# Sliding-window attention beside a squared-ReLU MLP: second products placed between first products, and attention values written to consecutive rows

## The chip, the cores and the metric

The kernel runs on one core of one Trainium2 chip, in float32 throughout; matrix products take their operands as pairs of a rounded high part and a low part. The metric is device time in microseconds. A core has five engines with instruction queues of their own: TensorE (PE in the profile; its weight loads are PEld), VectorE (DVE), ScalarE (ACT), GpSimd (POOL) and SyncE (SP). All transfers of this kernel are issued by SP, in program order.

## The reference

For 2048 tokens of 640 features, with 32 heads of 20 features and a window of 256 keys:

```python
xn = layernorm(x)
q, k, v = split(xn @ wqkv)                     # 32 heads, Dh = 20
scores = (q @ k.T) * 20 ** -0.5                # kept where 0 <= i - j < 256
s = (softmax(scores) @ v) @ wo
r = relu(xn @ w1 + b1)                         # F = 1536
g = silu((r * r) @ w2 + b2)
out = x + s * g
```

## The kernel before, in words

**Phase one** (to about 116 us of the profile) normalizes x, transposes it, spills it in halves (`xs`), forms all values V and the first group of queries and keys.

**The main loop** (L1133, to about 784 us) has 267 steps: 16 pairs of heads times 16 tiles of 128 queries, and 11 steps of lag. A step holds scores of one pair and tile (`sps`, L478), their row maxima on VectorE (L486), the transposed scores of nine steps earlier (`stps`, L518), their exponentials on ScalarE (`p`, L524) and the masks of these on GpSimd (L525, L527). Every fourth step also turns four tiles of row maxima (L493) on TensorE, rounds them on ScalarE (`row` L499, `mrow` L500), forms the low part on GpSimd (L501), and two DMAs write them into two rows of the queries (`qs<-mrow`, L503), so that the transposed scores come with the maximum already subtracted. Every fourth step also multiplies exponentials by V (`ops`, L546); the result goes through ScalarE (`osb`, L551) to DRAM (`o`, L552, issued at L564). The rest of TensorE's time is filled, from a generator, with other products: at first queries and keys (`qkps`), then the MLP.

**The MLP** runs in eight blocks: two halves of F times four groups of 512 tokens. A block has six first products (`hps`: `th` 0 and 1, two halves of the block's tokens, times `fp` 0 to 2) of 30 matmuls each, 256 columns wide, and eight second products (`yps`: tile `tt` 0 to 3 times half `nh` of the output features) of 18 matmuls each, 320 wide. A first product is evacuated by two relu (L930) and two squares (`hh`, L932) on ScalarE, two squares on VectorE that read the bank again (`sq`, L936), and two subtractions on GpSimd (`hl`, L937). A second product with `tt` 0 or 1 reads the three pairs (`hh`, `hl`) of `th` 0, for each half of F's chunks in the order `hh`, `hh`, `hl`. It leaves its bank by one addition on VectorE (L968); the tile goes to DRAM.

**Lanes and banks.** Every product is done in two halves of 64 rows of the array, which run beside each other: a front half of one product with a back half of the product before it. A half without a partner takes a slot alone. All products share three banks of PSUM. The back lane is a product behind the front lane, so a product's bank becomes free only when its back halves and its evacuation are done.

**What sets the order.** All engines' orders are as written by the program. A planner's clock adds up assumed costs of matmuls; `later(wait, f)` writes `f`'s instructions when that clock has advanced by `wait`; `ps.free(after)` says when a bank counts as free again; `room()` makes the filler wait for that. A second product is written once the piece it reads is in `made`, that is, once the instructions that make it have been written. Weight pieces (`wraw`) are loaded a few steps ahead and split on ScalarE (L767) and VectorE (L770); `ensure` (L738) forces what is not yet split. Bulk transfers (weights, `xb`, the next pair's queries and keys) go out at two places of a step, by `issue` (L671).

**The tail** (from 794 us) is the output projection (`wops`, L599): eight units of two tiles. For each unit, sums and unnormalized values come back from `o` (L1026, L1027) and `y` (L1029), VectorE divides (L1040, L1044), and the product is multiplied by the gate (`res`, L1098), added to x on GpSimd (L1103) and written out (`out_dram`).

## Time and profile before

| | |
|---|---|
| median of 3 runs | 875.52 us (875.32 to 877.31) |
| profiled execution | 873.83 us |
| its span | 872.1 us |
| granted TensorE clock, mean | 0.996 |
| TensorE busy | 853.6 us (98%), 10640 matmuls |
| VectorE, ScalarE, GpSimd busy | 497.1, 401.0, 332.0 us |
| DMA | 168.60 MB, mean 193 GB/s |

Times of single instructions come from one profiled execution. Matmuls overlap in TensorE's pipeline: the time from one start to the next counts, not the length of one. A row of the timeline gives start, length, engine, line, operation, output and inputs, and in brackets how long the engine was idle before it and what released it.

### The profile page before, as it was taken

How to read it: one execution, taken by the hardware profiler on the slowest of the kernel's cores; microseconds unless marked ns; L12 is line 12 of the kernel's file. 1: busy time of each engine (PE TensorE's matmuls, PEld its weight loads, DVE VectorE, ACT ScalarE, POOL GpSimd, SP SyncE). 2: the span in 40 equal slices, each digit the busy share in tenths (PEclk: the TensorE clock that was granted, in tenths of full speed). 3: DMA queues.
4: the chain of work that ended last, by engine and by line, in shares of the span. 5: the costliest groups of instructions: out<-in, count | busy, mean ns of one | idle time of the engine just before them, and what ended most of it. 6: DMA issues, size and time to landing. Idle time of an engine off the chain costs nothing.

```text
span 872.1 us, 26728 instructions
## 1 busy us (share of the span) xinstructions
PE 853.6 (98%) x10640; PEld 796.5 (91%) x10640; DVE 497.1 (57%) x1448; ACT 401.0 (46%) x800; POOL 332.0 (38%) x700
## 2 busy tenths in 40 slices
PE   9999999999999999999999999999999999999998
PEld 8999999888888999989989989998989999999998
DVE  7652146656567755555655566764655555536764
ACT  5222114545556744644644654743643644653231
POOL 6010002333333643643543543642543543541343
PEclk9999999999999999999999999999999999999999
DMA  7997578787788546245348346367348256157995
GB/s 268 310 399 276 173 205 264 252 256 232 256 275 287 128 144 177 70 138 187 78 129 249 85 114 182 98 196 214 85 129 244 81 148 200 50 163 236 288 296 172
DMA packets 92901, 168.60 MB, mean 193 GB/s; under 512 B 9448, under 2 KB 41320, under 8 KB 91752
## 3 DMA queue, kind: packets, MB, share of 16 engines
q1 hardware_dynamic: 92776, 166.89, 62.1%
q8 instruction: 84, 1.38, 0.7%
q14 instruction: 41, 0.34, 0.1%
HBM read 94.71 MB, written 71.57 MB: 191 GB/s over the span
## 4 chain that ended last, share of the span: by engine, by line
PE 86%; DMA 7%; DVE 2%; issue 2%; ACT 1%; POOL 1%; SPq 0%; DVEq 0%; POOLq 0%; ACTq 0%
PE yps L468 19%; PE hps L468 18%; PE qkps L468 13%; PE ops L546 9%; PE vps L228 8%; PE stps L518 5%; PE wops L599 4%; PE sps L478 4%; DMA qs<-mrow 4%; PE qkps L205 3%; DMA out_dram<-res 2%; DMA vp<-v_d 1%; POOL res L1103 1%; PE tps L172 1%; DVE junk L486 0%
## 5 line engine op out<-in xcount | busy, mean ns | idle before, releaser
L486 DVE CUSTOM_DVE_ANT_0 junk<-sps,mask 128x384 bf16<-128x384 f32 (+2 forms) x512 | 272.3, 532 | 211.4 <-PE sps L478 57.6
L524 ACT ACTIVATE p<-stps 128x768 f32<-128x768 f32 (+2 forms) x256 | 197.8, 773 | 291.8 <-PE stps L518 240.9
L468 PE MATMUL yps<-w,hh 64*128 64x320 f32 x1536 | 229.3, 310 | 5.1 <-DVE sq L936 4.7
L525 POOL TENSOR_SCALAR_AFFINE_SELECT p<-p 128x256 f32<-128x256 f32 x256 | 105.9, 414 | 333.0 <-ACT p L524 329.8
L468 PE MATMUL hps<-xb,w 64*128 64x256 f32 x2520 | 218.5, 284 | 0.0
L468 PEld LDWEIGHTS hps<-xb,w 64*128 64x128 f32 x2520 | 207.0, 188 | 5.5 <-issue 5.4
L468 PEld LDWEIGHTS yps<-w,hh 64*128 64x128 f32 x1536 | 181.5, 185 | 11.3 <-DVE sq L936 6.2
L468 PE MATMUL yps<-w,hl 64*128 64x320 f32 x768 | 172.4, 309 | 0.0
L478 PE MATMUL sps<-ks,qs 60*128 60x384 f32 (+2 forms) x512 | 140.9, 342 | 0.8 <-DVE mt L486 0.5
L518 PE MATMUL stps<-qs,ks 62*128 62x384 f32 (+2 forms) x512 | 132.8, 334 | 4.9 <-DMA qs<-mrow 4.8
L468 PEld LDWEIGHTS yps<-w,hl 64*128 64x128 f32 x768 | 112.3, 185 | 1.8 <-issue 1.7
L468 PE MATMUL qkps<-xT,wgkh 64*128 64x512 f32 x320 | 100.9, 395 | 0.0
L468 PE MATMUL qkps<-xT,wgqh 64*128 64x512 f32 x320 | 99.2, 393 | 0.0
L546 PE MATMUL ops<-p,vp 128*21 128x128 f32 (+1 forms) x2112 | 92.8, 313 | 0.0
L527 POOL TENSOR_SCALAR_AFFINE_SELECT p<-p 128x256 f32<-128x256 f32 x224 | 92.7, 414 | 0.0
L518 PEld LDWEIGHTS stps<-qs,ks 62*128 62x128 f32 x512 | 85.8, 188 | 7.4 <-issue 7.0
L478 PEld LDWEIGHTS sps<-ks,qs 60*128 60x128 f32 x512 | 86.0, 186 | 2.9 <-DVE mt L486 1.7
L546 PEld LDWEIGHTS ops<-p,vp 128*21 128x21 f32 x2112 | 65.2, 100 | 22.0 <-issue 8.8
L937 POOL TENSOR_TENSOR hl<-sq,hh 128x256 fp32r<-128x256 f32 x96 | 71.0, 756 | 24.5 <-ACT hh L932 21.9
L228 PE MATMUL vps<-wv,xT 128*128 128x320 f32 x480 | 71.5, 308 | 0.0
L228 PEld LDWEIGHTS vps<-wv,xT 128*128 128x128 f32 x480 | 70.5, 188 | 0.1
L599 PE MATMUL wops<-wo,oT 128*128 128x320 f32 x384 | 63.2, 314 | 2.1 <-DVE res L1098 1.4
(100 smaller groups left out, 1188.0 us busy)
## 6 DMA issues: line engine op xcount, KB each, us to landing
ks<-k_d SPq DMA_DIRECT2D x64, 240.0 KB
qs<-q_d SPq DMA_DIRECT2D x64, 240.0 KB
xb<-xs SPq DMA_DIRECT2D x60, 256.0 KB
xs<-xT SPq DMA_DIRECT2D x8, 1280.0 KB
y<-ysb SPq DMA_DIRECT2D x32, 320.0 KB
k_d<-shm SPq DMA_DIRECT2D x19, 512.0 KB
q_d<-shm SPq DMA_DIRECT2D x19, 512.0 KB
o<-osb SPq DMA_DIRECT2D x64, 128.0 KB
```

Source lines behind the costliest of these rows:

```text
L205: nc.tensor.matmul(ps, wt[:, c, :], xT[part][b][:, c * BT + t0:c * BT + t0 + n], start=m == 1, stop=m == 3 * KC)
L228: nc.tensor.matmul(ps, xT[xp][b][:, c * BT + t * P: c * BT + (t + 1) * P], wv[wp][:, c, nh * HALF:(nh + 1) * HALF], start=first and m == 0 ...
L468: return nc.tensor.matmul(out, a[r], b_[r], skip_group_check=True, **kw)
L478: nc.tensor.matmul(ss[hh][:, :nk], qs[i][o, q * P:(q + 1) * P], ks[i][o, k0 * P:k0 * P + nk], start=True, stop=True)
L486: nc.vector.tensor_tensor_reduce(out=junk[:, :nk], in0=ss[hh][:, :nk], in1=mask[:, 3 * P - nk:], scale=1.0, scalar=-3.0e38, op0=ALU.add, o ...
L518: nc.tensor.matmul(tps[:, hh, :n], ks[i][o, kb * P:(kb + 1) * P], qs[i][o, kb * P:kb * P + n], start=True, stop=True)
L524: nc.scalar.activation(p32[:, :, :n], tps[:, :, :n], AF.Exp, scale=SCALE)
L525: nc.gpsimd.affine_select(p32[:, :, 0:P], p32[:, :, 0:P], pattern=[[0, 2], [1, P]], compare_op=ALU.is_ge, fill=0.0, base=0, channel_multip ...
L527: nc.gpsimd.affine_select(p32[:, :, 2 * P:], p32[:, :, 2 * P:], pattern=[[0, 2], [-1, P]], compare_op=ALU.is_gt, fill=0.0, base=0, channel ...
L546: nc.tensor.matmul(ot[r0:r0 + VW, c0:c0 + len(part), :], vps[p][:, kb // 4, kb % 4, hh, :], pt[:, hh, :].rearrange("p (t n) -> p t n", n=P ...
L599: nc.tensor.matmul(ps, a, b_, start=j == 0, stop=j == n - 1)
L937: nc.gpsimd.tensor_sub(hh[1][:, sls[i]], sq, f32(hh[0][:, sls[i]]))
```

## The change

- **Order of products.** Before, a block had its six first products, then its eight second products. Now the second products of its first tile lie between the first products of its second pass: h(0,0), h(0,1), h(0,2), h(1,0), y(0,0), h(1,1), y(0,1), h(1,2), then y(1,0) to y(3,1). The forced splitting of w2 and the first loads of `yin` move with y(0,0), to a place two products earlier; `late` is called only from `tt` 1 on.
- **Both squares together.** The two `sq` and `hl` of a first product are written at one time, 0.8 after relu, in place of 0.6 and 1.0; the bank counts as free 1.0 later, in place of 0.7.
- **Rows of the output write.** `o` has the layout [16 pairs, 128 rows, 256], so that a write goes to 128 consecutive rows. In the tail, each unit's sums and values come by eight loads of 32 partitions in place of two of 128.
- **Bulk transfers.** The rule that held them back in every fourth step (up to the row-maximum DMAs) and in the step before it is gone; a piece of `xb` costs 0.4 of the rate, in place of 0.8.

```diff
-    o_d = [dram.tile([2 * 32, H, MT], F32, name=f"o_{g}") for g in range(NB)]
+    o_d = [dram.tile([NP, P, MT], F32, name=f"o_{g}") for g in range(NB)]
...
-            post(o_d[g][:, 2 * p:2 * p + 2, :].rearrange("r h n -> h r n"), osb.rearrange("p e n -> p (e n)"))
+            post(o_d[g][p], osb.rearrange("p e n -> p (e n)"))
...
     def issue(amount):
-        if state[2] % 4 == 3 or state[2] % 4 == 0 and not rowed[0]:
-            return
         credit[0] = min(credit[0] + amount, amount)
...
-        its = [bulk_dma(0.8, f32(xb[p])[:, c], xs_d[p][b][:, c]) for p in range(2) for c in cs]
+        its = [bulk_dma(0.4, f32(xb[p])[:, c], xs_d[p][b][:, c]) for p in range(2) for c in cs]
...
+            def first(th, fp):
...
                         def rest(i):
                             sq = at2.tile([P, MT], F32, tag="sq", name="sq")
                             nc.vector.scalar_tensor_tensor(sq, ps.tile[:, sls[i]], b1t[:, fi + i:fi + i + 1], rs[i], ALU.add, ALU.mult)
                             nc.gpsimd.tensor_sub(hh[1][:, sls[i]], sq, f32(hh[0][:, sls[i]]))
                             if i:
                                 made.add((th, fp))
-                                ps.free(0.7)
-                        later(0.6, lambda: rest(0))
-                        later(1.0, lambda: rest(1))
+                                ps.free(1.0)
+                        later(0.8, lambda: (rest(0), rest(1)))
...
-            if n % NB == 0:
-                ensure(f"2{hf}")
-            if n == NB:
-                load_yin(0)
-                load_yin(1)
-            wt2 = w2t[hf]()
-            for tt in range(4):
...
+            def second(tt, nh):
+                if (tt, nh) == (0, 0):
+                    if n % NB == 0:
+                        ensure(f"2{hf}")
+                    if n == NB:
+                        load_yin(0)
+                        load_yin(1)
+                    wt2[0] = w2t[hf]()
                 t = b * 4 + tt
+                yield from room()
+                if n == last and tt:
+                    late(2 * tt + nh)
...
+            for fp in range(NFH // 2):
+                yield from first(0, fp)
+            for fp in range(NFH // 2):
+                yield from first(1, fp)
+                if fp < 2:
+                    yield from second(0, fp)
+            for tt in range(1, 4):
                 for nh in range(2):
-                    yield from room()
-                    if n == last:
-                        late(2 * tt + nh)
-                    job = start(nh)
-                    for fc in range(NFH):
-                        yield from product(job, nh, fc)
+                    yield from second(tt, nh)
...
-        rows = o_d[u // 2][32 * (u % 2):32 * (u % 2 + 1)]
-        nc.sync.dma_start(sums, rows[DH].unsqueeze(0).to_broadcast([4, H, MT]))
-        nc.sync.dma_start(ob, rows[:DH].rearrange("(c k) h n -> (k h) c n", k=4))
+        rows = o_d[u // 2].rearrange("p (h r) n -> (p h) r n", h=2)[:, 32 * (u % 2):32 * (u % 2) + VW]
+        for k in range(4):
+            nc.sync.dma_start(sums[32 * k:32 * k + H], rows[:, DH])
+            nc.sync.dma_start(ob[32 * k:32 * k + H], rows[:, k:DH:4])
```

**TensorE at the end of a block's third first product.** Before, in the third block: `hps_6894` is that product, the two others are the next two. Its `hl` is `hl_7177`, read for the first time 173 rows further on.

```order
L468 MATMUL hps_6894<-xb0_1_6157,w1_0_1_3364 128x256
L468 MATMUL hps_7027<-xb0_1_6157,w1_0_2_3540 128x256
L468 MATMUL hps_6894<-xb1_1_6158,w1_0_1_3364 128x256
L468 MATMUL hps_7169<-xb0_1_6157,w1_0_0_3362 128x256
L468 MATMUL hps_6894<-xb0_1_6157,w1_0_2_3540 128x256
L468 MATMUL hps_7169<-xb1_1_6158,w1_0_0_3362 128x256
```

Now, in the same block, `hps_6928` is the third first product, `yps_7193` the first second product, and `hh_6955` and `hl_6956` belong to the block's first first product:

```order
L468 MATMUL hps_6928<-xb1_1_6328,w1_0_1_3364 128x256
L468 MATMUL yps_7193<-w2_0_0_3931,hh_6955 128x320
L468 MATMUL hps_6928<-xb0_1_6327,w1_0_2_3540 128x256
L468 MATMUL yps_7193<-w2_0_1_3933,hh_6955 128x320
L468 MATMUL yps_7193<-w2_0_0_3931,hl_6956 128x320
L468 MATMUL yps_7193<-w2_0_0_3931,hh_6955 128x320
```

The third row is the last half of `hps_6928`. Thirty-one rows further on, the same product reads what `hps_6928` leaves, `hh_7199` and `hl_7200`:

```order
L468 MATMUL yps_7193<-w2_0_1_3933,hh_7199 128x320
L468 MATMUL hps_7044<-xb0_1_6327,w1_0_1_3364 128x256
L468 MATMUL yps_7193<-w2_0_2_4087,hh_7199 128x320
L468 MATMUL hps_7044<-xb1_1_6328,w1_0_1_3364 128x256
L468 MATMUL yps_7193<-w2_0_1_3933,hl_7200 128x320
```

The distance from a third product's last half to the first use of its `hl` goes from 173 rows to 31, of which 14 are of `yps_7193`, the others back halves of `hps_7044` and one step's scores.

**ScalarE in the fifth block, where w2 of the second half of F is forced.** Before, the forced pieces (`w2_1_1`, L767) stand ahead of the sixth first product's relu:

```order
L524 ACTIVATE p32_9997<-stps_9988 128x768
L499 ACTIVATE row_10001<-stps_9988 8x128
L500 ACTIVATE mrow_10002<-row_10001 8x128
L767 ACTIVATE w2_1_1_9615<-raw_9783 128x640
L524 ACTIVATE p32_10063<-stps_10056 128x768
L767 ACTIVATE w2_1_1_9615<-raw_9813 128x640
L930 ACTIVATE relu_10090<-hps_9810,b1t_108 128x256
L930 ACTIVATE relu_10092<-hps_9810,b1t_108 128x256
```

Now three of them stand, with a row-maximum step, ahead of the third first product's relu (`hps_9730`), whose results y(0,0) reads next:

```order
L524 ACTIVATE p32_9960<-stps_9951 128x768
L499 ACTIVATE row_9964<-stps_9951 8x128
L500 ACTIVATE mrow_9965<-row_9964 8x128
L765 ACTIVATE w2_1_0_9636<-raw_9654 128x640
L765 ACTIVATE w2_1_1_9638<-raw_9839 128x640
L765 ACTIVATE w2_1_1_9638<-raw_9895 128x640
L927 ACTIVATE relu_9998<-hps_9730,b1t_108 128x256
L927 ACTIVATE relu_10000<-hps_9730,b1t_108 128x256
L929 ACTIVATE hh_9996<-relu_9998 128x256
L929 ACTIVATE hh_9996<-relu_10000 128x256
```

**SP at the start of the tail.** The last write of `o` and the first unit's loads, before:

```order
L1026 DMA sums<-o_85 128x1x256
L1027 DMA ob_14435<-o_85 128x5x256
L1029 DMA yb_14436<-y_84 128x2x640
L564 DMA o_86<-osb 2x64x256
L751 DMA raw<-in_A_wo_dram 32x640 x8
L877 DMA yin<-y_83 128x640
```

and now:

```order
L564 DMA o_86<-osb 128x256
L1027 DMA sums<-o_85 32x256
L1028 DMA ob_14486<-o_85 32x5x256
L1027 DMA sums<-o_85 32x256
L1028 DMA ob_14486<-o_85 32x5x256
L1027 DMA sums<-o_85 32x256
L1028 DMA ob_14486<-o_85 32x5x256
L1027 DMA sums<-o_85 32x256
L1028 DMA ob_14486<-o_85 32x5x256
L1030 DMA yb_14487<-y_84 128x2x640
```

The write's shape is 128x256 in place of 2x64x256, and a unit has nine loads in place of three.

More of the change, by code (lines that the diff above doesn't have):

```diff
@@ L665, in lin1 @@
         return tiles[t][:, o:o + n]
-    bulk, rowed = [], [False]
+    bulk = []
     credit = [0.0]
     def issue(amount):
-        if state[2] % 4 == 3 or state[2] % 4 == 0 and not rowed[0]:
-            return
         credit[0] = min(credit[0] + amount, amount)
@@ L988, in product @@
                     for hp, wp in ((0, 0), (0, 1), (1, 0)):
[L989 to L990 removed]
+                        m += 1
+                        halves(job, ps, hs[tt // 2, fc // 2][hp][:, fc % 2 * MT + tt % 2 * P:fc % 2 * MT + (tt % 2 + 1) * P], lin1(wt2[0], (wp * NFH + fc) * D + nh * HALF, HALF), m == 1, m == 3 * NFH)
                         yield 0.133
[L992 to L998 removed]
+            for fp in range(NFH // 2):
[5 more added lines that the diff above has]
+            for tt in range(1, 4):
+                for nh in range(2):
+                    yield from second(tt, nh)
             if n < last and nxt:
@@ L1133, in attn_mlp_kernel @@
         for s in range(steps):
-            state[2], rowed[0] = s, False
+            state[2] = s
             vload[0] = 0.2 * (s % 4 == 0) + 0.5 * (s % 4 == 3)
```

97 lines of the change are left out of this document (45 added, 52 removed).

## The prediction

> **What bounds the kernel now.** I read the page first, then the waits, then stretches of the timeline. The page (busy time per engine, then the granted clock and DMA share in 40 slices):
>
> ```profile
> PE 853.6 (98%) x10640; PEld 796.5 (91%) x10640; DVE 497.1 (57%) x1448; ACT 401.0 (46%) x800; POOL 332.0 (38%) x700
> PEclk9999999999999999999999999999999999999999
> DMA  7997578787788546245348346367348256157995
> ```
>
> TensorE is busy 98% of 872.1 us at nearly full clock. Nothing else is near a bound on average; DMA reaches it only in the last slices. So an edit can pay only by removing TensorE gaps, half-filled slots or a slow clock, and costs by adding them. The waits (engine, line waited for: us in total, times, longest) say which gaps there are:
>
> ```profile
> PEld yps L468 <- DVE sq L936: 6.2, 6, 1.5
> PE yps L468 <- DVE sq L936: 4.7, 5, 1.3
> PEld yps L468 <- DVE ysb L968: 1.7, 5, 0.6
> PE yps L468 <- DVE ysb L968: 0.3, 1, 0.3
> PEld stps L518 <- issue: 7.0, 8, 1.8
> PE stps L518 <- DMA qs<-mrow: 4.8, 6, 1.6
> DVE res L1098 <- DMA out_dram<-res: 9.6, 6, 4.2
> PE wops L599 <- DVE res L1098: 1.4, 3, 0.8
> ```
>
> Gap A is a second product (yps) waiting for a bank that first products (hps) leave: between 5.0 (matmul rows) and 7.9 us (weight-load rows); I take 7. Gap B is the transposed scores (stps) waiting for the row maxima that come back by DMA: between 4.8 and 7.0; I take 6. Gap C is in the output projection, 1.4 us or somewhat more; I take 1.5.
>
> One A in full, on ScalarE, VectorE and TensorE (start, us, engine, what; in brackets the idle time before it):
>
> ```profile
> 503.93 0.28 PE L468 MATMUL hps<-xb,w 64*128 64x256 f32 x1
> 504.66 0.81 ACT L524 ACTIVATE p<-stps 128x768 f32<-128x768 f32 x1 [1.01 <-PE stps L493]
> 505.37 0.25 ACT L499 ACTIVATE row<-stps 8x128 f32<-8x128 f32 x1
> 505.65 0.31 ACT L500 ACTIVATE mrow<-row 8x128 fp32r<-8x128 f32 x1
> 505.87 0.81 ACT L930 ACTIVATE relu<-hps,b1t 128x256 f32<-128x256 f32 x2
> 507.40 1.42 POOL L937 TENSOR_TENSOR hl<-sq,hh 128x256 fp32r<-128x256 f32 x2 [0.68 <-ACT hh L932]
> 507.71 0.56 PE L468 MATMUL yps<-w,hh 64*128 64x320 f32 x4 [1.27 <-DVE sq L936]
> ```
>
> The last hps half starts at 503.93, but its relu starts 1.94 us later, behind the exponentials and the two row-maximum pieces of that step.
>
> One B, and what stands ahead of it in the DMA queue (SP rows; windows with PE, PEld, DVE, ACT, POOL busy, granted clock, DMA share, GB/s):
>
> ```profile
> 314.75 0.54 SPq L564 DMA_DIRECT2D o<-osb  x1
> 317.22 1.43 SPq L503 DMA_DIRECT2D qs<-mrow  x2
> 315.90:319.30 3.40, 3.40 (x51) 3.40 (x50) 1.66 (x7) 2.08 (x4) 1.30 (x4) 1.00 0.14 41
> 605.42 0.44 PE L518 MATMUL stps<-qs,ks 62*128 62x384 f32 x2 [1.60 <-DMA qs<-mrow]
> 606.50:610.00 3.50, 3.50 (x36) 3.41 (x34) 0.94 (x3) 1.09 (x3) 0.77 (x2) 0.51 0.46 109
> ```
>
> The output write of the attention values, 128 KB, is alone in flight in the first window: 0.14 of 16 engines is 2.2 engines, 41 GB/s, so 128 KB needs about 3.2 us. The small row-maximum DMA is queued behind it. The worst B (1.6 us before 605.42) is followed by 3.5 us at half clock (0.51): 1.7 us more lost.
>
> **The change, part by part.** The sum is made against the profiled execution, 873.8 us (span 872.1 and 1.7 outside it); the median of the runs is 875.5, 1.7 above it, and I add that at the end.
>
> *Rows of the output write.* From 2x64x256 to 128x256: with more engines it no longer blocks the row maxima. B goes from 6 to 0.3 (what is left where transfers of xb now precede it): **-5.7**. If the write stays as it is, 0; if all goes, -7.0. The stretch at half clock behind the worst B goes with it: -1.7.
>
> The Trainium skill, DMA: Bandwidth & Descriptors, section "Why a DMA increments its semaphore by 16 and not by 1", says that a DMA runs on the largest k up to 16 that divides the slowest dimension of both sides: 2 before and 16 now. The 2.2 engines above agree. By that rule 128 KB would take an eighth of its 3.2 us, and B goes wholly; by the row alone I could not tell how many engines the new shape gets.
>
> *Order of products: bank waits.* Alternating kinds removes most hand-overs from hps to yps with a long evacuation. In the new order two stay right behind a row-maximum step, at about 1.4 each (as the 1.27 above), four smaller ones at about 0.35, and the yps-to-yps ones stay at 1.0: 5 in place of 7, **-2** (-4 if the small ones vanish, 0 if none shrinks).
>
> *Order of products: the new wait.* The first second product of a block now starts when the third first product has only just ended. Its 15th front half reads hl of that product, 14 halves after that product's last half on TensorE. What a second-product half costs in a slot of its own (chain of waits, then two timeline pieces with their successors):
>
> ```profile
> 785.87 7.54 PE yps L468 x76
> 788.28 0.56 PE L468 MATMUL yps<-w,hh 64*128 64x320 f32 x4
> 788.57 0.42 PE L468 MATMUL yps<-w,hl 64*128 64x320 f32 x2
> 788.72 0.56 PE L468 MATMUL yps<-w,hh 64*128 64x320 f32 x4
> 790.15 0.45 PE L468 MATMUL yps<-w,hh 64*128 64x320 f32 x2
> 790.44 0.31 PE L468 MATMUL yps<-w,hl 64*128 64x320 f32 x1
> 790.59 0.45 PE L468 MATMUL yps<-w,hh 64*128 64x320 f32 x2
> ```
>
> Six halves in 0.44 us when paired (788.28 to 788.72), three when alone (790.15 to 790.59): 0.147 a slot either way. So 14 slots are 2.06 us, with one pair of scores 2.2. How long hl takes, at its quickest, and what a forced weight piece takes:
>
> ```profile
> 437.76 0.28 PE L468 MATMUL hps<-xb,w 64*128 64x256 f32 x1
> 438.07 0.84 ACT L930 ACTIVATE relu<-hps,b1t 128x256 f32<-128x256 f32 x2 [0.25 <-PE hps L468]
> 439.65 0.74 POOL L937 TENSOR_TENSOR hl<-sq,hh 128x256 fp32r<-128x256 f32 x1 [0.36 <-ACT hh L932]
> L767 ACT ACTIVATE w<-raw 128x640 fp32r<-128x640 f32 x12 | 8.7, 726 | 0.0
> ```
>
> From the last half's start (437.76) to the end of the first hl (440.39) is 2.63 us: 0.4 more than the 2.2 there are. The second hl half takes another 0.74, and is read only 0.44 later: 0.7 in all at the quickest. In blocks 3, 5 and 7 a whole row of attention work lies between (some 4 us), and nothing waits. The five others, by what stands ahead of relu on ScalarE: block 1 nothing, 0.7; block 0 the exponentials (0.7) and the values' copy (0.3), 1.5; blocks 2 and 6 a row-maximum step as at 504.66, where hl came 4.18 after the last half (503.93 to 508.11), of which the new place is 0.7 later in the step, 1.2 each; block 4 the same and three forced pieces of w2 (3 x 0.73), 3.4. Together **+8.0**. From below: only the 0.4 five times, +2; from above: eight blocks at the 504.66 case without its 0.7 (4.2 - 2.2 = 2.0), +16. I take 8, since the order gives each block's queue. Behind the waiting half are queued all of TensorE's work, its back lane too: scores, row maxima and exponentials of the next step are late by the same, so it's paid in full. The 3.4 in block 4 is more than the stall that went before 606.5, so I expect a stretch at half clock behind it: +1.7, which cancels the one removed.
>
> Page TensorE: Matmul & The Clock Gate of the Trainium skill, Part 1 on the HAM clock gate, asks for an idle window of about 3.4 us before the clock halves. The trace differs: 1.6 us idle came before the 0.51 at 606.5. By the rule the stall in block 4 is just long enough for one such stretch, and the sum would be the same.
>
> *Order of products: lanes.* A half without a partner takes the slot of two. After the last values there were 77 halves in 50 slots (7.54 us); by the new order 100 halves in 68: 18 x 0.147 = +2.6. In the loop 35 more halves are alone (+2.3), and 20 of yps move out to the end (-1.5): +0.8. **+3.4**; if partners turn up, 0.
>
> *Both squares together, bank said free later; gate on bulk transfers gone.* One VectorE piece earlier, one bank promise 0.3 later: no term but those above. Transfers of xb now precede the row-maximum DMAs in four steps; that's in the 0.3.
>
> *Tail loads.* A unit's two loads become eight. SP rows of unit three, and C's place:
>
> ```profile
> 816.13 0.54 SPq L1026 DMA_DIRECT2D sums<-o  x1
> 816.77 0.51 SPq L1027 DMA_DIRECT2D ob<-o  x1
> 827.63 0.49 DVE L1098 TENSOR_TENSOR res<-wops,yb 128x320 f32<-128x320 f32 x1 [1.04 <-DMA out_dram<-res]
> SPq L1063 <- POOL res L1103: 33.2, 7, 5.5
> 820.00:850.00 30.00, 29.16 (x196) 28.37 (x194) 20.76 (x29) 8.83 (x10) 12.25 (x12) 1.00 0.98 302
> ```
>
> Eight issues for two are at most 6 x 0.54 = 3.2 us more on SP, which sits idle there 33.2 us in seven waits for GpSimd, 4.7 each: hidden; without that cover 3.2 a unit would delay the output writes. DMA is full (0.98), and the output writes land late for VectorE (1.04 before 827.63). The sums are read to four copies; if they spread like the other loads the queue is shorter and C goes: **-1.5** (0 to -2).
>
> Sum: -5.7 -1.7 -2 +8.0 +1.7 +3.4 -1.5 = +2.2: 876.0 in a profiled execution, **877.7 as the median**.
>
> **The rivals.** *Slower, by the wait for hl.* If hl is late in all eight blocks by an average of 1.6 (between 0.7 and 2.0), that's 12.8, 4.8 more than my term: 882.5. For it: VectorE holds the row maxima ahead of sq. Against it: the 4 us in three blocks. It decides from 0.4 us beyond my 8.0, since 878.1 is 0.3% over 875.5.
>
> *Faster: hl is hardly waited for.* If what stands ahead of relu is done by then, because earlier stalls let ScalarE catch up, 2.5 remains of 8.0, and no slow clock follows: 877.7 - 5.5 - 1.7 = 870.5. For it: ScalarE is 46% busy. Against it: relu was late by 1.94 at 505.87.
>
> *The tail loads are slower.* The new loads read 1 KB pieces at a distance of 64 KB. If they take twice as long, the full DMA queue gives back what the sums save; C stays: 879.2.
>
> The Trainium skill's DMA page, section "Latency and other measured facts", reports copies slowed at row pitches of 512 KiB and above that are powers of two. The pitch here is smaller; no run shows it yet.
>
> *The row maxima stay late.* With the gate gone, xb transfers go out right ahead of them: at four steps 1 us each, 4: 881.7.
>
> **How the numbers follow.** Forecast 0.42, slower by hl 0.22, faster 0.19, tail loads 0.09, maxima late 0.08. About 0.3% (2.6 us) is what a measurement can tell from no change: 872.9 to 878.1. Faster: 0.18 of the faster case and 0.03 of the forecast, **0.21**. Same: 0.28 of the forecast, 0.01, 0.02, 0.04 and 0.02 of the others, **0.37**. Slower: 0.11, 0.20, 0.05 and 0.06, **0.42**. The forecast's own range is 874 to 881; with the other cases' centres and a little beyond, **870 to 884**.
>
> **What would show it.** In the changed profile: no wait of stps for qs<-mrow above 0.5 us, and the lone write's window at a DMA share far above 0.14; waits of yps for POOL's hl (or ScalarE's hh) of about 8 us in five places, the longest in block 4 with a clock near 0.5 behind it; waits of yps for sq of about 4; about 10 us of yps after the last values; DVE's wait for out_dram under 3 us. It is wrong if the hl waits are under 4 or over 11, or if stps still waits 4 us.

## The result

The changed kernel is slower: median 897.1 us of 4 runs (893.7 to 901.9) against 875.4 (874.3 to 877.3) for the kernel before, a ratio of 1.0261 (95% interval 1.0233 to 1.0289). The forecast was 877.7, the range 870 to 884. The profiled execution took 893.7, its span is 892.0; it was 872.1.

The page of the changed kernel (busy time, granted clock and DMA share in 40 slices):

```profile
PE 863.2 (97%) x10640; PEld 801.1 (90%) x10640; DVE 495.7 (56%) x1448; ACT 399.9 (45%) x800; POOL 329.8 (37%) x700
PEclk9999999999999999999999999999999999998999
DMA  7996678779788263174265345274275263066995
```

The same matmuls, and a place near the end where the clock dips and TensorE is less than full. The waits on the way, as they were shown for the kernel before:

```profile
PEld yps L468 <- DVE sq L933: 7.2, 12, 1.4
PE yps L468 <- DVE sq L933: 3.7, 7, 1.1
PEld yps L468 <- DVE ysb L967: 8.5, 4, 7.6
PE yps L468 <- DVE ysb L967: 7.6, 2, 7.4
PEld yps L468 <- POOL hl L934: 8.3, 12, 1.8
PE yps L468 <- POOL hl L934: 5.9, 7, 1.6
DVE res L1099 <- DMA out_dram<-res: 9.3, 6, 4.4
PE wops L599 <- DVE res L1099: 3.5, 5, 0.8
```

Transposed scores no longer wait for the row maxima (no such line is left). The waits for hl are there, 5.9 us by TensorE's matmul rows and 8.3 by its weight-load rows. New and not forecast is one wait of 7.4 us for `ysb`, the addition that empties a second product's bank. On VectorE and TensorE (in brackets the idle time before):

```profile
789.94 0.81 DVE L774 TENSOR_TENSOR wo<-raw,wo 128x640 fp32r<-128x640 f32 x1
796.00 0.83 DVE L774 TENSOR_TENSOR wo<-raw,wo 128x640 fp32r<-128x640 f32 x1 [5.24 <-ACT wo L773]
796.74 1.75 DVE L1041 RECIPROCAL sums<-sums 128x256 f32<-128x256 f32 x1
802.38 0.96 DVE L109 TENSOR_TENSOR oT<-ob,oT 128x768 fp32r<-128x768 f32 x1 [0.91 <-ACT oT L108]
803.25 0.82 DVE L774 TENSOR_TENSOR wo4l<-raw,wo4h 128x640 fp32r<-128x640 f32 x1
803.99 0.88 DVE L967 TENSOR_TENSOR ysb<-yps,yin 128x320 f32<-128x320 f32 x2
804.53 0.90 PE L468 MATMUL yps<-w,hh 64*128 64x320 f32 x4 [7.38 <-DVE ysb L967]
```

VectorE is idle for 5.24 us, waiting for a piece of wo; then it divides the tail's first unit (796.74 to 803.3) and splits the last piece of wo; only then does the addition run, and TensorE goes on. In the kernel before, the addition that mattered stood ahead of the division:

```profile
784.10 0.49 DVE L968 TENSOR_TENSOR ysb<-yps,yin 128x320 f32<-128x320 f32 x1 [2.15 <-PE yps L468]
785.24 1.75 DVE L1040 RECIPROCAL sums<-sums 128x256 f32<-128x256 f32 x1
791.76 0.88 DVE L968 TENSOR_TENSOR ysb<-yps,yin 128x320 f32<-128x320 f32 x2
```

The windows of the changed kernel (stretch, length, then PE, PEld, DVE, ACT, POOL busy, granted clock, DMA share, GB/s) show the stall, a slow clock behind it, and the tail:

```profile
793.50:804.60 11.10, 3.72 (x42) 3.45 (x39) 6.96 (x9) 4.44 (x6) 0.00 (x0) 0.86 0.76 232
804.60:812.76 8.16, 7.43 (x48) 6.93 (x49) 1.40 (x4) 0.95 (x1) 0.00 (x0) 0.77 0.26 83
812.76:890.00 77.24, 72.06 (x480) 70.37 (x480) 49.06 (x69) 18.48 (x21) 30.25 (x30) 1.00 0.86 247
```

By stage, from the profiled executions (start of the span to the last matmul of the values, from there to the first `wops`, the tail to the span's end):

| | before | changed | difference | forecast |
|---|---|---|---|---|
| to the last values | 785.6 | 792.1 | +6.5 | +1.1 |
| last values to the tail | 8.5 | 20.7 | +12.2 | +2.6 |
| tail | 78.0 | 79.2 | +1.2 | -1.5 |

So three fifths of the loss lie in the few microseconds ahead of the tail.

### The profile page after: what moved, and what is told of

It reads as the page before. It is cut to its first block, busy times and chain, and to the rows that moved or that the text cites. A ratio compares the mean times of both kernels' runs of the same rounds, so it can differ in the third digit from the quotient of the medians.

```text
span 892.0 us, 26811 instructions
## 1 busy us (share of the span) xinstructions
PE 863.2 (97%) x10640; PEld 801.1 (90%) x10640; DVE 495.7 (56%) x1448; ACT 399.9 (45%) x800; POOL 329.8 (37%) x700
## 4 chain that ended last, share of the span: by engine, by line
PE 85%; DMA 4%; issue 3%; POOL 2%; DVE 2%; ACT 2%; SPq 2%; POOLq 0%; DVEq 0%; ACTq 0%
PE yps L468 19%; PE hps L468 18%; PE qkps L468 13%; PE ops L546 10%; PE vps L228 8%; PE stps L518 5%; PE sps L478 4%; PE qkps L205 3%; PE wops L599 3%; DMA out_dram<-res 2%; DMA sums<-o 1%; DVE sq L933 1%; ACT p L524 1%; POOL res L1104 1%; PE tps L172 1%
## 5 line engine op out<-in xcount | busy, mean ns | idle before, releaser
L468 PE MATMUL yps<-w,hh 64*128 64x320 f32 x1536 | 272.7, 314 | 12.8 <-DVE ysb L967 7.6
L468 PE MATMUL hps<-xb,w 64*128 64x256 f32 x2520 | 255.0, 284 | 0.0
L468 PEld LDWEIGHTS hps<-xb,w 64*128 64x128 f32 x2520 | 238.5, 188 | 4.9 <-issue 4.7
L525 POOL TENSOR_SCALAR_AFFINE_SELECT p<-p 128x256 f32<-128x256 f32 x256 | 105.3, 411 | 345.3 <-ACT p L524 334.0
L468 PEld LDWEIGHTS yps<-w,hh 64*128 64x128 f32 x1536 | 206.1, 187 | 21.8 <-DVE ysb L967 8.5
L468 PE MATMUL yps<-w,hl 64*128 64x320 f32 x768 | 193.5, 314 | 5.9 <-POOL hl L934 5.9
L478 PE MATMUL sps<-ks,qs 60*128 60x384 f32 (+2 forms) x512 | 138.3, 342 | 0.4 <-DVE mt L486 0.4
L468 PEld LDWEIGHTS yps<-w,hl 64*128 64x128 f32 x768 | 121.3, 187 | 10.7 <-POOL hl L934 8.3
L527 POOL TENSOR_SCALAR_AFFINE_SELECT p<-p 128x256 f32<-128x256 f32 x224 | 91.0, 406 | 0.0
L478 PEld LDWEIGHTS sps<-ks,qs 60*128 60x128 f32 x512 | 83.9, 186 | 3.1 <-DVE mt L486 1.6
```

Source lines behind the costliest of these rows:

```text
L468: return nc.tensor.matmul(out, a[r], b_[r], skip_group_check=True, **kw)
L478: nc.tensor.matmul(ss[hh][:, :nk], qs[i][o, q * P:(q + 1) * P], ks[i][o, k0 * P:k0 * P + nk], start=True, stop=True)
L525: nc.gpsimd.affine_select(p32[:, :, 0:P], p32[:, :, 0:P], pattern=[[0, 2], [1, P]], compare_op=ALU.is_ge, fill=0.0, base=0, channel_multip ...
L527: nc.gpsimd.affine_select(p32[:, :, 2 * P:], p32[:, :, 2 * P:], pattern=[[0, 2], [-1, P]], compare_op=ALU.is_gt, fill=0.0, base=0, channel ...
```

## The experiments

Each was timed beside the kernel before on its chip. Stages as above; "halves" are the second-product halves that TensorE still had to do after the last values.

| | median | ratio (95%) | to last values | to the tail | halves | tail |
|---|---|---|---|---|---|---|
| before | 874 to 875 | | 785.6 | 8.5 | 77 | 78.0 |
| changed | 897.1 | 1.0261 (1.0233 to 1.0289) | 792.1 | 20.7 | 100 | 79.2 |
| e1_late_load | 897.5 | 1.0246 (1.0204 to 1.0288) | 795.0 | 20.1 | 100 | 80.9 |
| e2_last_block_old | 886.2 | 1.0122 (1.0078 to 1.0167) | 790.0 | 12.2 | 100 | 81.3 |
| e3_old_order | 877.4 | 1.0027 (1.0007 to 1.0047) | 778.8 | 17.9 | 89 | 79.6 |
| e4_rows_only | 868.5 | 0.9939 (0.9915 to 0.9964) | 776.1 | 8.5 | 77 | 82.0 |
| f1_division_behind | 894.6 | 1.0218 (1.0186 to 1.0250) | 790.9 | 17.3 | 100 | 82.9 |
| f2_two_writes | 864.2 | 0.9870 (0.9840 to 0.9899) | 776.2 | 8.5 | 77 | 78.1 |
| f3_no_gate | 874.6 | 1.0007 (0.9979 to 1.0035) | 785.3 | 8.5 | 77 | 76.8 |
| f4_squares_together | 882.3 | 1.0081 (1.0049 to 1.0113) | 786.5 | 17.6 | 89 | 77.3 |
| g1_shifted | 878.7 | 1.0053 (1.0029 to 1.0077) | 776.1 | 17.2 | 99 | 81.2 |
| g2_order_only | 911.9 | 1.0409 (1.0361 to 1.0457) | 822.4 | 10.1 | 79 | 79.0 |
| g3_order_five_blocks | 898.7 | 1.0275 (1.0231 to 1.0319) | 810.1 | 10.5 | 87 | 77.0 |
| g5_squares_addition_first | 876.5 | 1.0025 (1.0002 to 1.0048) | 790.2 | 10.9 | 89 | 78.5 |
| h1_shifted_division_behind | 870.3 | 0.9959 (0.9935 to 0.9984) | 776.2 | 10.8 | 99 | 79.3 |
| h2_changed_squares_apart | 889.4 | 1.0167 (1.0136 to 1.0197) | 795.1 | 10.1 | 79 | 82.6 |
| h3_two_writes_eight_loads | 868.8 | 0.9937 (0.9917 to 0.9956) | 776.5 | 8.5 | 77 | 81.3 |

### Four first runs

The first theory after the result was a queue on SP: the tail's first load of `ob` held SP for 8 us in the changed kernel, with the last pieces of wo behind it (SP's own waits):

```profile
SPq L1028 <- PE stps L518: 8.0, 1, 8.0
```

```diff
         def late(j):
-            load(0)
+            if j >= 3:
+                load(0)
```

> The changed kernel with one edit: the loads of the tail's first unit are written two second products later (from y(1,1) on, in place of y(1,0)). Theory Q (a queue is blocked): in the changed kernel SP stands 8.0 us on the first unit's load of ob, which waits for a buffer that first product h(1,2) still reads; the last pieces of wo, queued behind it on SP, come late, their split on VectorE comes late, and the addition behind it that frees a bank; so TensorE idles 7.4 us and then runs at half clock for about 2. Q expects that stall under 1 us and 884 to 888. Rival L (the eight small loads themselves are slow): no change, 893 to 902. Rival H (waits for hl and the forced pieces of w2 are what costs): no change, 893 to 902.

The base of the first three of these runs is the changed kernel. Nothing moved: 897.5, and TensorE still waited 6.4 us there. The load was written later and SP's wait for it fell from 8.0 to 2.3 us, but the last pieces of wo were late all the same. The theory in this form fell.

```diff
-                if n == last and tt:
+                if n == last:
...
+            mixed = n < last
...
-                if fp < 2:
+                if mixed and fp < 2:
                     yield from second(0, fp)
-            for tt in range(1, 4):
+            for tt in range(mixed, 4):
```

> The changed kernel with the old order of products in the last of the eight blocks alone. Q: there are again eight second products behind the block's last first product, so the stall goes, and the 23 halves more that are left at the end go too: 881 to 885. L: the loads are as before in number, 893 to 902. H: one wait for hl of 1.6 us less, 892 to 900.

886.2, a little above the 881 to 885 of theory Q and below the other two; the stretch ahead of the tail is 12.2 in place of 20.7, and the wait 0.8 in place of 7.4. So the loads themselves don't make the stall (they are the same here), and the order in the last block has a part in it. The halves didn't fall to 77, as expected, but stayed at 100: the order in the last block is not what leaves them. Nor does their number alone make the stall, since with 100 halves only 0.8 us of it is left here; what else decides it wasn't worked out.

```diff
-                if n == last and tt:
+                if n == last:
...
+            mixed = False
...
-                if fp < 2:
+                if mixed and fp < 2:
                     yield from second(0, fp)
-            for tt in range(1, 4):
+            for tt in range(mixed, 4):
```

> The changed kernel with the old order of products in all blocks; the rows of the output write, both squares together, the tail's eight loads and the bulk transfers stay changed. Q and H: the waits of the transposed scores (5.3 us) and the half clock behind the longest (1.7) are gone, the waits for banks are back, so 867 to 872. L: over 876, since the loads stay.

877.4: missed by theories Q and H, and the most useful of the four. The time is the one that rival L gave, but most of the loss isn't L's, the slow loads: the tail is 1.6 us longer than before, the stretch ahead of it 9.4. The loop is 6.8 us shorter than before, as the rows promised, but the stall ahead of the tail is there without the new order, 5.92 us:

```profile
787.97 0.90 PE L468 MATMUL yps<-w,hh 64*128 64x320 f32 x4 [5.92 <-DVE ysb L967]
```

```diff
-    o_d = [dram.tile([2 * 32, H, MT], F32, name=f"o_{g}") for g in range(NB)]
+    o_d = [dram.tile([NP, P, MT], F32, name=f"o_{g}") for g in range(NB)]
...
-            post(o_d[g][:, 2 * p:2 * p + 2, :].rearrange("r h n -> h r n"), osb.rearrange("p e n -> p (e n)"))
+            post(o_d[g][p], osb.rearrange("p e n -> p (e n)"))
...
```

The base is the kernel before; the eight loads of the tail go with it.

> The kernel before with the new rows of the output write and the tail's eight loads alone. If the write on few engines is what made the transposed scores wait: 867 to 871, no wait of stps for qs<-mrow over 0.5 us. If the held-back bulk transfers matter as well: 871 to 875. L: slower than 876.

868.5, faster than before by 0.6%. The loop gains 9.5 us and no transposed score waits for `qs<-mrow`, as forecast. But the tail is 4.0 us longer. So e3, which has this and the two remaining parts without the order, loses 9 us against e4 to one of them: the bulk transfers or the squares.

### The squares, alone, and the addition behind the division

```diff
-                                ps.free(0.7)
-                        later(0.6, lambda: rest(0))
-                        later(1.0, lambda: rest(1))
+                                ps.free(1.0)
+                        later(0.8, lambda: (rest(0), rest(1)))
```

> The kernel before, with both squares written together and the bank said free 0.3 later: nothing else. Theory D: the planner falls behind by some ten halves, so that at the end of the loop the addition of a second product is written behind the division of the tail's first unit, as in the changed kernel: a stall of 5 to 7 us there, 880 to 885. If squares only shift bank waits: 873 to 877.

882.3: this small edit alone costs 8 us, all of it in the stretch ahead of the tail (17.6 in place of 8.5), and the old loads are in place. The base is the kernel before. VectorE and TensorE of that run:

```profile
789.18 1.75 DVE L1039 RECIPROCAL sums<-sums 128x256 f32<-128x256 f32 x1
794.82 0.96 DVE L109 TENSOR_TENSOR oT<-ob,oT 128x768 fp32r<-128x768 f32 x1 [0.91 <-ACT oT L108]
795.70 0.88 DVE L967 TENSOR_TENSOR ysb<-yps,yin 128x320 f32<-128x320 f32 x2
796.24 0.90 PE L468 MATMUL yps<-w,hh 64*128 64x320 f32 x4 [6.49 <-DVE ysb L967]
```

and its window there:

```profile
790.00:800.00 10.00, 3.76 (x34) 3.77 (x36) 4.94 (x7) 4.02 (x4) 0.00 (x0) 0.66 0.70 214
```

89 halves are left instead of 77. The division of the tail's first unit is written at a fixed product, as soon as the loop is over. The explanation tested next is this: with 12 halves more to do, the addition for an earlier product isn't written yet at that point, and lands behind the division. The last product's first half waits for that bank. The granted clock falls to 0.66 in those 10 us. To test just this:

```diff
             if j >= 5:
+                finish()
                 turn_out(0, 0)
```

> The run with both squares together, with one edit: before the division of the tail's first unit is written, additions that are due are written. Theory D (the addition that frees the last product's bank stands behind the division): the stall of 6.7 us goes, 873 to 878. If the stall has another cause, it stays: 880 to 885.

876.5, from 882.3. With the addition written first, the stretch is 10.9 in place of 17.6. That settles in the old order that the addition's place in VectorE's queue makes the stall; why it falls there was not tested. (The profiled execution of this run took 881, so its stages stand a little high.)

The same in the changed kernel takes a later division, since there the product's back halves too are written behind it:

```diff
                 yield from room()
-                if n == last and tt:
-                    late(2 * tt + nh)
                 sl = slice(nh * HALF, (nh + 1) * HALF)
                 ps = Acc(HALF, "yps")
+                if n == last and tt:
+                    late(2 * tt + nh)
...
-            if j >= 5:
+            if j >= 7:
                 turn_out(0, 0)
-            if j >= 6:
+            if j >= 7:
                 turn_out(0, 1)
```

> The changed kernel with one edit: in the last block the division of the tail's first unit is written one or two products later, behind the addition that frees the bank for the last second product. Theory D (a queue of VectorE in the wrong order): with 100 halves instead of 77 left after the last values, that addition is written only after the division (about 6.5 us on VectorE), so the last product's first half waits for the whole division; here the addition is ahead of it. D expects the stall of 7.4 us down to under 2 (the fourth piece of wo still stands ahead) and 886 to 890. If SP's wait for the buffer of ob is what makes the stall, it stays above 5 and the time above 893.

894.6: it took away only 2.5. The wait before the last product fell under 2, as theory D expected, but the time is the one expected of its rival, over 893: the tail now waits for the division itself:

```profile
796.56 0.82 DVE L774 TENSOR_TENSOR wo<-raw,wo 128x640 fp32r<-128x640 f32 x1 [6.99 <-ACT wo L773]
797.30 0.48 DVE L967 TENSOR_TENSOR ysb<-yps,yin 128x320 f32<-128x320 f32 x1
797.84 0.56 PE L468 MATMUL yps<-w,hh 64*128 64x320 f32 x4 [1.87 <-DVE ysb L967]
808.22 3.54 PE L599 MATMUL wops<-wo,oT 128*128 128x320 f32 x12 [4.52 <-DVE ysb L967]
```

1.87 + 4.52 in place of 7.38. In the new order wo is split late: its buffers open when the block's last first product is done, and that product now has two second products ahead of it. The first piece of wo is split at 786.6 in the changed kernel and at 771.1 before, while the loop ends only 6.5 us later. So the order adds its own lateness in the last block (in e2, with the old order there, the first piece is split at 777.6), and the squares the wrong place in VectorE's queue.

### The order, shifted, alone, and with the squares apart

```diff
                 yield from first(1, fp)
-                if fp < 2:
-                    yield from second(0, fp)
+                if fp > 0:
+                    yield from second(0, fp - 1)
```

> The changed kernel with the two second products of the first tile one place later: h(0,0), h(0,1), h(0,2), h(1,0), h(1,1), y(0,0), h(1,2), y(0,1). If the wait for hl is a matter of the distance between the third first product and y(0,0), it goes wholly in all blocks (7.0 us) and with it the half clock behind block 4 (1.7); the block's last first product also ends some 5 us earlier, so the buffers of wo open earlier and the wait at the end is shorter, though the addition still stands behind the division: 880 to 887. If the hl waits only move to another product: 892 to 898.

878.7, a little better than expected: one place later, and the loop falls from 792.1 to 776.1 us. No wait of TensorE for hl is left in this run. What remained was the stall at the end, 4.61 us, and the tail. With the later division of f1 on top:

> The run with the second products one place later, with the division of the tail's first unit written behind the addition that frees the bank for the last second product. In that order the pieces of wo are split in time, so nothing else stands ahead of the division. Theory D: the stall of 4.8 us goes, and at most 2 of it comes back as a wait at the start of the tail: 874 to 877 from 878.7. If the stall has another cause: 878 or more.

```profile
777.70 0.83 DVE L774 TENSOR_TENSOR wo4l<-raw,wo4h 128x640 fp32r<-128x640 f32 x1 [2.54 <-ACT wo4h L773]
778.44 0.49 DVE L967 TENSOR_TENSOR ysb<-yps,yin 128x320 f32<-128x320 f32 x1
778.84 1.75 DVE L1041 RECIPROCAL sums<-sums 128x256 f32<-128x256 f32 x1
786.90 1.99 PE L599 MATMUL wops<-wo,oT 128*128 128x320 f32 x12 [0.68 <-DVE ysb L967]
```

870.3, better than expected, and faster than the kernel before. The addition at 778.44 stands ahead of the division, the pieces of wo were there in time, and no stall is left: of g1's 17.2 us, 10.8 remain. The whole change with its two mistakes mended thus gives 0.996 of the time before. That is no better than the rows alone (e4, 0.994, with the same loop of 776 us): mended, the order adds nothing to them.

The changed kernel with the squares as they were:

```diff
-                                ps.free(1.0)
-                        later(0.8, lambda: (rest(0), rest(1)))
+                                ps.free(0.7)
+                        later(0.6, lambda: rest(0))
+                        later(1.0, lambda: rest(1))
```

> The changed kernel with one edit: the squares apart again and the bank said free 0.3 earlier, as before. If the squares alone decide what is written behind the division: the stall at the end falls under 2 and the time to 884 to 890. If it is the late end of the block's last first product (two second products go ahead of it), the stall or a wait for wo's pieces stays: 892 to 900. If the order only works with the squares together, it gets worse, as with the order alone: over 900.

889.4, just inside the first case. The stall goes, as that case said: 79 halves and 10.1 us ahead of the tail. But the loop is 3 us longer than in the changed kernel: with the squares apart, TensorE waits more for `sq` (10.2 against 7.2 us by weight loads). So in the new order the squares together are worth 3 us in the loop and cost 10.6 at its end.

> The kernel before with the new order of products alone (squares apart, old rows, held-back bulk transfers). If the parts add up: the changed kernel lies 23 over before, of which the runs with single parts give -5.6 (rows), 0.7 (bulk) and 8.3 (squares), so the order is worth +20: 890 to 897. If the squares' stall at the end and the order's are the same one, the sum counts it twice or the order alone has it: between 885 and 893.

The edit is the function `first` and `second` and their order, and nothing else of the change. 911.9, worse than any expectation. The waits show what was not thought of:

```profile
PEld hps L468 <- DMA xb<-xs: 11.2, 6, 3.2
PE hps L468 <- DMA xb<-xs: 9.4, 4, 3.0
PE yps L468 <- POOL hl L936: 6.5, 10, 1.1
```

The next block's first products wait for xb. A block's last first product ends later, so xb's buffers open later; that they then fill too slowly by the old rule for bulk transfers fits, for TensorE has this wait in none of the runs with the new order and the new rule (h2, with the squares apart as here, among them). No run changes the rule alone in the new order.

The last run with the order is built on two writes (below), with `finish()` as in g5:

```diff
+            mixed = n not in (0, NB, last)
...
+                if mixed and fp < 2:
+                    yield from second(0, fp)
+            for tt in range(mixed, 4):
```

> The run with two writes, with the new order in blocks 1, 2, 3, 5 and 6 alone (old order in those that force w2 and in the last), and additions that are due written ahead of the division. If the order gains bank waits where nothing is forced: 860 to 864. If the hl waits and lone halves cost more than it saves (hl 3.5 of the 7.0, lone halves 1): 865 to 869.

898.7: missed for the same reason, with waits for xb of 11.4 us. It says nothing of what it was made for.

### The write's rows, the bulk transfers and the tail's loads

```diff
-            post(o_d[g][:, 2 * p:2 * p + 2, :].rearrange("r h n -> h r n"), osb.rearrange("p e n -> p (e n)"))
+            for h in range(2):
+                post(o_d[g][:, 2 * p + h, :], osb[64 * h:64 * (h + 1)].rearrange("p e n -> p (e n)"))
```

> The kernel before, with the write of the attention values as two writes of 64 rows each to the old layout; the tail's loads stay as before. If the number of engines of the write is all that kept the row maxima late, the loop gains as in the run with the new rows alone (9.5 us up to the last values) and the tail keeps its old 78 us: 864 to 867. If a write of 64 rows is no better spread than before: 873 to 877.

864.2, as forecast, and the fastest version of the study: 0.987 of the time before. It keeps the old layout and the old loads; the write goes out in two halves of 64 rows. Windows of the write that was shown of before, from its first data to its last: in the changed kernel (issued at 314.05, with a row of the idle time behind it), then in this run (the first half issued at 313.34), and of this run's tail:

```profile
314.80:315.40 0.60, 0.60 (x14) 0.60 (x12) 0.38 (x3) 0.21 (x1) 0.00 (x0) 1.00 0.65 219
315.40:315.75 0.35, 0.35 (x10) 0.35 (x8) 0.22 (x2) 0.35 (x1) 0.00 (x0) 1.00 0.00 0
```

```profile
314.45:315.65 1.20, 1.20 (x19) 1.20 (x18) 0.32 (x4) 1.14 (x3) 0.29 (x1) 1.00 0.51 109
784.62:862.70 78.08, 73.02 (x480) 71.90 (x480) 49.17 (x69) 18.49 (x21) 30.31 (x30) 0.98 0.82 260
```

The write of 128 KB that moved for 3.4 us at 41 GB/s moves for 0.6 us at 219 GB/s when it goes to 128 rows, and for 1.2 at 109 in two halves. The mean share of the 16 DMA engines goes from 0.14 to 0.65 and 0.51. The loop gains 9.5 and 9.4 us; the tail is unchanged here, 78.1.

```diff
-        if state[2] % 4 == 3 or state[2] % 4 == 0 and not rowed[0]:
-            return
...
-        its = [bulk_dma(0.8, f32(xb[p])[:, c], xs_d[p][b][:, c]) for p in range(2) for c in cs]
+        its = [bulk_dma(0.4, f32(xb[p])[:, c], xs_d[p][b][:, c]) for p in range(2) for c in cs]
```

> The kernel before, without the rule that holds bulk transfers back, xb at 0.4: nothing else. If the rule's removal is harmless: 873 to 877. If xb transfers now go out ahead of the row maxima, each time stps waits 1 us or more: 878 to 884.

874.6, no difference. Alone, the bulk rule is neutral; g2 and g3 suggest that the new order needs it.

The run with two writes, with eight loads a unit in the tail:

```diff
-        nc.sync.dma_start(sums, rows[DH].unsqueeze(0).to_broadcast([4, H, MT]))
-        nc.sync.dma_start(ob, rows[:DH].rearrange("(c k) h n -> (k h) c n", k=4))
+        for k in range(4):
+            nc.sync.dma_start(sums[32 * k:32 * k + H], rows[DH])
+            nc.sync.dma_start(ob[32 * k:32 * k + H], rows[k:DH:4].rearrange("c h n -> h c n"))
```

> The run with two writes and the old layout, with the tail's sums and values fetched by eight loads of 32 partitions a unit, as in the changed kernel, but from rows that lie side by side (1 KB pieces without gaps between heads) in place of 64 KB apart. The tail is 78.1 us with two loads and 82.0 with the new rows and eight loads. If the number of issues costs the 4 us: 82 here, 866 to 870. If the distance of the rows costs them: 78 here, 862 to 866.

868.8. The tail is 81.3 us: it is the number of loads that costs, 3.3 of the 4.0 us, and not mainly the distance of the rows. TensorE's waits for `res`, those of `res` for its buffer and SP's idle time for GpSimd in that run, then the last two in its base, the run with two writes:

```profile
PE wops L600 <- DVE res L1100: 4.8, 9, 0.8
DVE res L1100 <- DMA out_dram<-res: 9.1, 7, 4.4
SPq L1065 <- POOL res L1105: 11.8, 7, 5.5
```

```profile
DVE res L1099 <- DMA out_dram<-res: 5.8, 4, 4.1
SPq L1064 <- POOL res L1104: 33.7, 7, 5.5
```

In the base, as in the kernel before, TensorE waited for `res` some 1.4 us in two or three places; here it is 4.8 in nine. The loads use up most of SP's idle time, and VectorE waits 3.3 us more for output writes. That these go out later because eight loads are issued between them fits, but wasn't tested.

The price is higher than it looks. The base's tail has a stretch at a slow clock (0.98 in its window, about 1.6 of 78 us), and the tails of e4 and of this run have none (1.00). With the clock at 1.00 a tail with two loads a unit took 76.8 us (f3), with eight 79.2 (changed kernel), 79.3 (h1), 81.3 (h3) and 82.0 (e4): 2.4 to 5.2 us for the loads. What makes this spread isn't known.

## Why the prediction was wrong, step by step

*What bounds the kernel, and the row maxima behind the output write: right.* Forecast -5.7 and -1.7 for the half clock; the rows alone (f2, e4) gave 9.4 to 9.5 us in the loop. The write now moves for 0.6 us in place of 3.4, at 219 GB/s in place of 41. The rule of the Trainium skill (DMA: Bandwidth & Descriptors, section "Why a DMA increments its semaphore by 16 and not by 1"), by which 16 engines would share the new write, is borne out in its sign and most of its size: a bit over fivefold here, where the prediction worked out eightfold from it. A small misreading beside it: DMA's share reaches 0.9 in the second and third slice of the page too, not only in the last ones.

*The new wait for hl: right in mechanism; the sum is right by luck.* Forecast 8.0 us in five blocks; TensorE waited 5.9 to 8.3, and one place later in the order it was gone (g1). But it waited in seven blocks, and blocks 5 and 7, in which nothing was to wait, have the two longest waits, 3.1 of the 5.9 us:

```profile
631.27 0.41 PE L468 MATMUL yps<-w,hl 64*128 64x320 f32 x1 [1.60 <-POOL hl L934]
763.94 0.41 PE L468 MATMUL yps<-w,hl 64*128 64x320 f32 x1 [1.47 <-POOL hl L934]
```

The five blocks that were named have 2.8 of their 8.0 by the matmul rows, so these were over-sized and two were missing. Block 4 had its forced pieces ahead of relu, as expected, but lost 1.9 us in four short stalls in place of 3.4, and had a slow clock behind. ScalarE and TensorE there, and the clock:

```profile
558.18 1.98 ACT L765 ACTIVATE w<-raw 128x640 fp32r<-128x640 f32 x3
560.06 0.80 ACT L927 ACTIVATE relu<-hps,b1t 128x256 f32<-128x256 f32 x2
561.22 0.41 PE L468 MATMUL yps<-w,hh 64*128 64x320 f32 x1 [0.79 <-ACT hh L929]
562.54 0.63 PE L468 MATMUL yps<-w,hl 64*128 64x320 f32 x1 [0.76 <-POOL hl L934]
```

```profile
560.00:570.00 10.00, 8.44 (x113) 7.54 (x113) 4.95 (x15) 3.83 (x9) 2.89 (x6) 0.83 0.50 141
```

0.83 in 10 us is the forecast 1.7. Not forecast: the slow stretch came behind a string of stalls of at most 0.8 us each, not behind one long one.

*Bank waits: wrong.* -2 was forecast; the weight loads' wait for `sq` went from 6.2 to 7.2 us and spread from 6 places to 12. The order alone does the opposite of what was forecast: 10.2 us with the squares apart (g2, h2). It is the squares together that lower this wait, to 3.2 in the old order (f4, e3).

*Lanes: the count right by luck, its cause and the loop's part wrong.* 100 halves were left, as the order said. But without the squares together it leaves 79 (h2), against 77 before; the squares leave 89 in the old order (f4), and both together 100. In the loop 0.8 was forecast for lone halves (by the prediction's own slot it should read 1.1: 35 times half of 0.147 is 2.6, not 2.3). The loop grew by 6.5 where 1.1 was forecast, although the rows gave 2 more than their term. Against e3, which differs by the order alone, it is 13.3 us longer, where the order's terms for the loop add up to 8.5. TensorE's matmul rows show about 9 of the 13.3 as waits for hl, hh, forced pieces and banks; the rest stands in no row of waits, and that it is lone halves and short gaps wasn't shown.

*"Both squares together, bank said free later: no term but those above": this is the step that failed.* Alone it costs 8 us (f4). With it 12 more halves are left at the loop's end, and an addition on VectorE moves from ahead of the tail's first division to behind it; TensorE stands still for 6.5 us, and the clock falls. With the addition ahead again 5.8 of the 8 are gone (g5). The working had asked what is queued behind the wait for hl, but for the end of the loop it looked only at TensorE's order. VectorE's, read at the same place, has the division ahead of the addition. In the changed kernel the new order adds late pieces of wo (f1, e2): the stall is 7.4 us, and with the slow clock behind it 9.3 of the 12.2; the other 2.9 are near the 2.6 that was forecast for the lone halves. Why the planner falls 12 halves behind was not tried, nor which of the edit's two parts does it, the squares' place or the later promise of the bank. This step is not the whole miss: without it the changed kernel still takes 889.4 (h2), above the range. The rest is the order's price in the loop, and putting the two second products one place later removes 16.0 us there (g1), though the waits for hl and the slow clock were sized at 9.7 together.

*Tail loads: "hidden" was wrong.* SP's idle time of 33.2 us did not cover the loads. They made the tail 3.3 us longer by their number, 4.0 with the new rows (h3, e4), where -1.5 was forecast. The changed kernel's tail is only 1.2 longer; 1.6 more is hidden in that, because the slow clock lies ahead of it and no longer in it (1.00 in its window; 0.98 before). The rest of the distance to e4 isn't explained. The prediction named the price for lost cover, but took the cover as a sum over the tail. The rival that the rows' distance of 64 KB slows the loads explains at most 0.7 (e4 against h3). The Trainium skill's figures for row pitches (DMA: Bandwidth & Descriptors, section "Latency and other measured facts") start at 512 KiB, and nothing here speaks against them.

*Bulk transfers: neutral alone, as said, but it seems needed by the order.* That its term may depend on another part was missed (g2, g3). The parts without the order do add up: -0.6%, +0.1% and +0.8% give e3's +0.3%. With the order the sum fails: g2's expectation, 890 to 897 by adding up, met 911.9.

*The rivals.* Slower by hl, at 882.5, came nearest, for the wrong reason. None had a queue in the wrong order at the loop's end.

## What to carry to other kernels

Where instructions are written by a planner, an edit of a few tenths of a microsecond in one of its times can turn round two pieces of work at a seam of the program; compare the order on every engine there, and look first for the instruction that frees a buffer behind one that merely prepares the next stage. Put a consumer as far behind its producer as the whole evacuation takes, counted with what stands ahead of it in each queue; here one product was the difference between 792 and 776 us. And take the part that pays by itself: writing the same rows in two halves gave more than the whole change, mended or not.

## What was not expected of the hardware

The length of a stall alone does not tell whether the clock falls. Several short stalls in a row were followed by a slow clock, 0.83 over 560 to 570 us, with no idle time above 0.8 us shown in that stretch; the one stall of 7.38 us was followed by 0.77 over the next 8.2 us. A single stall of 1.60 us came before the half clock at 606.5 in the kernel before, but the one of 1.60 us at 631.27 in the changed kernel left the clock full:

```profile
631.00:641.00 10.00, 9.73 (x145) 8.91 (x147) 5.04 (x16) 4.22 (x10) 5.01 (x11) 1.00 0.16 45
```

The Trainium skill (TensorE: Matmul & The Clock Gate, Part 1 on the HAM clock gate) puts an idle window of about 3.4 us ahead of the half rate; the stall of 7.38 agrees with it, and the string of short ones has no such window.

The same write of 128 KB moved at 41 GB/s as 2x64x256, at 109 as two times 64x256 and at 219 as 128x256. Small loads of 32 partitions, eight instead of two a unit, lengthened a tail of eight units by 3.3 us although their issuing queue had been idle for 33.7 us of it; 11.8 of these were left.
